# Attention and a gated layer on one core: conversion and attention steps at new places beside chunk 0's first layer, four transfers on GpSimd's queue, and a few sums of weights moved

## The chip, the cores and the metric

The kernel runs on one core of a Trainium2 chip. The metric is the time of one execution on the device, in microseconds. A run of the kernel before takes 1005.83 us (median of 3). The engines are called PE (TensorE), ACT (ScalarE), DVE (VectorE), POOL (GpSimd) and SP (SyncE); each works through its own queue in order.

## The reference

```python
def _attn_ref(q, k, v, g_norm):                       # 8 batches, 8 heads, 576 rows, 64 columns
    kv = np.einsum('bhsd,bhse->bhde', k, v)
    out = np.einsum('bhsd,bhde->bhse', q, kv)
    rms = np.sqrt(np.mean(out * out, axis=-1, keepdims=True) + 1e-06)
    return out / rms * g_norm

def _moe_ref(x, w_gate, w_val, w_out):                # 4608 tokens, 512 wide, 1536 inner
    gate = 1.0 / (1.0 + np.exp(-(x @ w_gate)))
    return (gate * (x @ w_val)) @ w_out
```

The attention's output, brought to 4608 rows of 512, is the `x` of the second part. The weights of the second part come as 64-bit floating point numbers and are read as integers; the kernel turns them into 32-bit floats itself.

## The kernel before

The 4608 tokens are worked on in nine chunks of 512. In each chunk the first layer makes `h` (gate times value, 12 blocks of 128 inner columns) and the second layer makes the output. Chunk 0 does this with plain matrix products. Chunks 1 to 8 use a fast multiplication with fewer products: 26 products for each of three blocks `j` in the first layer (78 in all, `first_layer_fast`, line 957) and 26 in the second (`second_layer_fast`, line 1059). It needs sums of the operands: of `x` (`x_sum`, lines 855 and 857, DVE), of the first layer's weights (`w1_sums(j)`, line 751, 28 sums on POOL for each `j`), of `h` (`h_sums`, line 733, POOL and partly DVE), and of w_out (`w_form(n)`, lines 1030 and 1032, 768 columns each, on DVE or POOL). These sums of weights are made once, beside chunk 0 and chunk 1, and those of the first layer are copied out to memory (`keep_w1`, line 768, one transfer per product, SP's queue) because later chunks load them from there (line 780).

**Chunk 0's first layer.** Its blocks 1 to 11 are 88 "places": place `p` is matmul `p % 8` of block `p // 8 + 1`, each a product of 128x128 by 128x512, which the trace lists as two instructions of line 599. Beside these matmuls a table called `places` hangs other work: `22:CV,CV,C` means that after the matmul of place 22 two conversion steps and the step `C` are issued. Within a place the order is: the matmul, then at the block's places 0 and 2 the two closing steps of the block before (`late`: a sigmoid on ACT called the gate, line 604, and a multiplication on DVE called `end`, line 607), then the steps of the table. As every engine takes its instructions in the order in which they are issued, the table decides what stands ahead of what on ACT, DVE, POOL and SP.

The steps' names:

- `CV` is the next conversion step. Each unit of weights (1024 columns) takes five, on DVE: c`u`.0 (line 197) and c`u`.1 (line 212), each followed by an activation on ACT (lines 202 and 217), then c`u`.2 (224), c`u`.3 (228) and c`u`.4 (235, or 237 for w_out). c`u`.2 needs the first activation, c`u`.3 the second. Some steps also issue a load of later weights on SP's queue. Block `u` of chunk 0 needs unit `u`; units 12 to 17 are w_out, and their remaining steps are issued in chunk 0's second layer (line 833), three in four matmuls.
- `LL` and `LL2` load K and V of batches 1 and 2 into `h_more` (`load_late`, line 134 for the eight large transfers, line 139 for the four small ones of the last 64 rows).
- `KV` and `KV2` multiply K by V of batches 1 and 2 (lines 389 and 396) into a PSUM tile `at`, of which there is one; `C` and `D` copy to `kvq`, `ASIDE` copies `KV2`'s result from PSUM to `kv_ahead` (line 400, ACT).
- `Q0`, `Q1` load q of batch 1 (lines 119 and 120, POOL's queue). `t00` to `t11` turn q on DVE (lines 408 and 410); `t11` issues the twelve q transfers of batch 2 on SP's queue.
- `au`, `asq`, `as0`, `as1`, `art`, `arc`, `an0`, `an1`, `an2`, `ax0`, `ax1` are the attention of the first four heads of batch 1: matmuls into `at` (line 439), square (ACT, 444), two sums (DVE, 447), root (ACT, 450), reciprocal (DVE, 483/485), three groups of six scalings (ACT, 479), two turns (DVE, 462 and 464) with their transfers (SP, 473). `bu` to `bx1` are the same for the other four heads.
- `W0` and `W1` are `w1_sums(0)` and `w1_sums(1)`. They write partly over `h_more`, which `KV2` reads. `w1_sums(2)` follows at the end of the conversions.

In chunk 1 the forms of w_out are issued at fixed products, from a list of (product, form, on POOL or not): `at1` counts the products of the first layer (0 to 77), `at2` those of the second (0 to 25). Form 22 is written over the slots 12 to 14 of block 1's first-layer sums, form 23 into a tile that the profile calls `w_ring`.

Of the kernel before, what the change touches and what calls it, by code (L numbers as in the profile page):

```python
# [20 lines left out]
def kernel(  # L21
# [11 lines left out]
    nc = tc.nc  # L33

    B, H, S, HD = q.shape
# [9 lines left out]
    PH = P // 2  # L45
# [19 lines left out]
    GH = G // 2  # L65
# [59 lines left out]
    def load_late(b):  # L125


        if b >= B:
            return
        mains = {}  # L130
        for n in range(NHP):
            for name, src in (("k", k), ("v", v)):
                mains[n, name] = t = kv_place(len(mains))
                nc.sync.dma_start(out=t.rearrange("p (h c) -> p h c", h=2),  # L134
                                  in_=src[b, 2 * n:2 * n + 2, 0:S4].rearrange("h (p j) d -> p h (j d)", j=NK4))
        rest = kv_place(len(mains))
        for i, src in enumerate((k, v)):
            for r in range(2):
                (nc.sync if b == 1 else nc.scalar).dma_start(out=rest[PH * r:PH * r + PH, GH * i:GH * i + GH].rearrange("p (h d) -> p h d", d=HD),
                                  in_=src[b, NHP * r:NHP * r + NHP, S4:S].rearrange("h p d -> p h d"))  # L140
        kv_late[b] = mains, rest

# [381 lines left out]
    def kv_place(i):  # L524
        return h_more.rearrange("p j s c -> p (j s c)")[:, G * i:G * i + G]
# [98 lines left out]
    KV, KV_OUT, Q, Q_OUT, U, U_SQUARE, U_SUM, U_ROOT, U_NORM, X, X_OUT = range(11)  # L624
# [157 lines left out]
    def w1_form(c, j, part, v):  # L782
        if c == 1:
# [11 lines left out]
    spare_sg = sgs.pop()  # L795
    batch1, second_batch = feed(1), feed(2)
    named = {"LL": lambda: load_late(1), "LL2": lambda: load_late(2), "KV": batch1[0][0], "KV2": second_batch[0][0],
             "W0": lambda: w1_sums(0), "W1": lambda: w1_sums(1),
             "ASIDE": second_batch[0][2], "CV": convert_step}
# [4 lines left out]
    for i, which in enumerate("ab"):  # L804
# [1 line left out]
            named[which + step] = batch1[1][2 * NRUN + 11 * i + n]  # L806
    places = """
        1:CV,CV 2:CV,Q0 4:CV,CV 5:CV,CV 6:CV,LL 7:CV,CV 10:CV,CV 11:Q1 15:CV 16:CV,CV 17:t00
        18:CV,CV 19:t01 20:KV 22:CV,CV,C 25:CV 26:CV,CV 29:au,LL2 30:CV
        31:asq 32:CV,t10,as0 34:CV,as1,art 35:CV 36:t11,arc,an0 37:an1 38:CV,an2 40:CV,CV 41:CV,ax0  # L810
        43:ax1 44:KV2,ASIDE 46:CV,W0 47:bu 48:CV,CV,bsq 50:CV,bs0 52:CV,CV 54:bs1 55:CV,CV,brt,D 57:CV,CV 58:CV 60:CV,brc
        62:bn0,bn1 63:bn2 64:CV 65:CV,CV,CV 66:CV,CV 67:CV 71:bx0 72:CV 74:W1 75:bx1
        80:CV,CV,CV,CV,CV 84:CV 87:CV,CV
    """
    at_place = {}
    for some in places.split():
        p, names = some.split(":")
# [45 lines left out]
    def x_sum(c, n):  # L863
        if c not in x_ops:
            x_ops[c] = x_sums(c)
        x_ops[c][n]()
# [160 lines left out]
    def w_form(v, eng, at_once=True):  # L1027
        sx_, x, sy, y = next(s_[1:] for s_ in W_SUMS if s_[0] == v)
        if sx_ > 0:
            eng.tensor_tensor(out=W_AT[v], in0=W_AT[x], in1=W_AT[y], op=op_of(sy))  # L1030
        else:
            nc.vector.scalar_tensor_tensor(out=W_AT[v], in0=W_AT[x], scalar=-1.0, in1=W_AT[y], op0=ALU.mult,
                                           op1=op_of(sy))
        if v not in STAY:
            stores.append(lambda: nc.sync.dma_start(out=kept3[STREAM.index(v)].rearrange("p (j n) -> p j n", j=N3),
                                                    in_=W_AT[v]))
            if at_once:
                stores.pop()()

    def second_layer_fast(c, at):  # L1040
# [62 lines left out]
        for i in range(1, NPR):  # L1103
            if i != 3:
# [8 lines left out]
                else:  # L1113
                    product(i, blocks)
                    finish(i)
        load_late(c + 2)

    fill.extend(x_early)
# [13 lines left out]
    for c in range(1, NG):  # L1132
        at1, at2 = {}, {}
        for p, step in x_late:
            at1.setdefault(p, []).append(step)
        x_late = []
        if c + 1 < B:
            kv, first_, then = second_batch if c == 1 else feed(c + 1)
            for p, step in (list(zip((21, 22) if c == 2 else (19, 20), kv)) if c > 1 else []) + first_:
                at1.setdefault(p, []).append(step)  # L1140
            for p, step in zip((3, 6) if c == 1 else (4, 6), then):
                at2.setdefault(p, []).append(step)
        if c + 1 < NG:
            for n, p in enumerate(X1 if c == 1 else X2 if c + 1 < B else X3):
                step = lambda n=n, c=c: x_sum(c + 1, n)
                if p < NPR:
                    at2.setdefault(p, []).append(step)
                else:
                    x_late.append((p - NPR, step))
        if c == 1:  # L1150
            for at_, forms in ((at1, ((28, 9, 0), (30, 10, 0), (34, 12, 0), (52, 11, 1), (57, 14, 0), (58, 8, 1), (61, 19, 0), (64, 16, 1))), (at2, ((1, 13, 0), (2, 22, 0), (3, 23, 1), (4, 25, 1), (9, 15, 0), (10, 24, 0), (10, 20, 0), (11, 17, 0), (12, 18, 0), (13, 21, 0)))):
                for p, n, pool_ in forms:
                    at_.setdefault(p, []).append(lambda n=n, eng=nc.gpsimd if pool_ else nc.vector, at_once=at_ is at1 or n == 13: w_form(n, eng, at_once))
        first_layer_fast(c, at1)
        if c == 1:
            sgs += [spare_sg] + more_sgs
        second_layer_fast(c, at2)
# [30 lines left out]
```

## Time and profile before

| | us |
|---|---|
| runs | 1005.83, 1005.03, 1005.9 |
| profiled execution, its own time | 1004.44 |
| its span, first to last instruction | 1002.7 |
| PE busy | 993.8 |
| PEld (weight loads) busy | 815.8 |
| DVE busy | 722.1 |
| ACT busy | 342.5 |
| POOL busy | 617.5 |

The granted clock of TensorE is 1.000 over the whole span. Chunk 0's first layer runs from 22 to 115 us of the span, its second layer to 158 us, chunk 1 to 263 us. In a timeline a row gives the start, the length, the engine, the line, the operation, output and inputs, and in brackets how long the engine had stood idle and who ended that. Rows that follow each other closely with equal names are merged (`x16`). A row of an engine with a `q` (ACTq, SPq, POOLq) is its queue's, which issues transfers.

### The profile page before, as it was taken

How to read it: one execution, taken by the hardware profiler on the slowest of the kernel's cores; microseconds unless marked ns; L12 is line 12 of the kernel's file. 1: busy time of each engine (PE TensorE's matmuls, PEld its weight loads, DVE VectorE, ACT ScalarE, POOL GpSimd, SP SyncE). 2: the span in 40 equal slices, each digit the busy share in tenths (PEclk: the TensorE clock that was granted, in tenths of full speed). 3: DMA queues.
4: the chain of work that ended last, by engine and by line, in shares of the span. 5: the costliest groups of instructions: out<-in, count | busy, mean ns of one | idle time of the engine just before them, and what ended most of it. 6: DMA issues, size and time to landing. Idle time of an engine off the chain costs nothing.

```text
span 1002.7 us, 16624 instructions
## 1 busy us (share of the span) xinstructions
PE 993.8 (99%) x5958; PEld 815.8 (81%) x5958; DVE 722.1 (72%) x1198; ACT 342.5 (34%) x606; POOL 617.5 (62%) x988
## 2 busy tenths in 40 slices
PE   8999999999999999999999999999999999999998
PEld 7455447888888888888888888888888888888887
DVE  4989999889757756784677676866587566755672
ACT  4566332562144213530344124421342133213320
POOL 1509997798359633965186707861595449744963
PEclk9999999999999999999999999999999999999999
DMA  9995414673799568846875577755864555444514
GB/s 271 269 265 183 172 51 115 215 236 127 248 301 272 176 189 240 239 156 203 257 240 171 181 223 237 203 171 179 258 201 141 167 173 211 156 149 162 214 53 122
DMA packets 156114, 195.43 MB, mean 195 GB/s; under 512 B 84832, under 2 KB 128864, under 8 KB 156032
## 3 DMA queue, kind: packets, MB, share of 16 engines
q0 software_dynamic: 22000, 114.11, 34.4%
q1 hardware_dynamic: 126864, 78.16, 27.6%
q10 hardware_dynamic: 7168, 2.10, 0.9%
q8 instruction: 47, 0.77, 0.3%
q14 instruction: 35, 0.29, 0.1%
HBM read 160.50 MB, written 25.56 MB: 186 GB/s over the span
## 4 chain that ended last, share of the span: by engine, by line
PE 73%; POOL 2%; DMA 1%; issue 0%; SPq 0%; DVE 0%; POOLq 0%
PE mm L957 46%; PE mm L1059 24%; PE at L439 1%; POOL h L733 1%; PE at L389 1%; DMA h_more<-in_v_dram 1%; POOL w_ring L1030 0%; POOL h_more L733 0%; PE at L396 0%; SPq L134 0%; POOL w L780 0%; DVE sg L927 0%; POOLq L780 0%; POOLq L1030 0%
## 5 line engine op out<-in xcount | busy, mean ns | idle before, releaser
L957 PE MATMUL mm<-xs,w 128*128 128x256 f32 x1428 | 331.8, 380 | 0.0
L957 PEld LDWEIGHTS mm<-xs,w 128*128 128x128 f32 x1428 | 270.5, 190 | 37.1
L957 PE MATMUL mm<-xT,w 128*128 128x256 f32 x948 | 229.8, 380 | 0.0
L957 PEld LDWEIGHTS mm<-xT,w 128*128 128x128 f32 x948 | 179.5, 190 | 25.0 <-issue 0.5
L780 POOL DMA_DIRECT2D w<-kept x84 | 46.8, 557 | 189.4 <-PE mm L957 187.3
L927 DVE TENSOR_TENSOR sg<-sg,mm 128x512 f32<-128x512 f32 (+1 forms) x176 | 100.7, 599 | 85.5 <-PE mm L957 41.5
L1059 PE MATMUL mm<-w,h 128*128 128x256 f32 x630 | 143.1, 379 | 0.3 <-POOL h L733 0.3
L1059 PEld LDWEIGHTS mm<-w,h 128*128 128x128 f32 x630 | 119.6, 190 | 17.0 <-POOL h L733 0.7
L919 POOL TENSOR_TENSOR h<-h,sg 128x512 f32<-128x512 f32 x72 | 96.0, 1350 | 57.0 <-DVE h L927 31.0
L923 ACT COPY temps<-mm 128x512 f32<-128x512 f32 (+1 forms) x128 | 66.0, 538 | 186.9 <-PE mm L1059 94.7
L733 POOL TENSOR_TENSOR h<-h 128x128 f32<-128x128 f32 x216 | 112.1, 531 | 16.6 <-DVE h_more L733 13.1
L1059 PE MATMUL mm<-w,h_more 128*128 128x256 f32 x474 | 108.2, 379 | 0.0
L916 ACT ACTIVATE sg<-sg 128x512 f32<-128x512 f32 x96 | 59.7, 630 | 131.5 <-DVE sg L927 131.5
L1059 PEld LDWEIGHTS mm<-w,h_more 128*128 128x128 f32 x474 | 90.1, 190 | 12.2
L923 ACT COPY sg<-mm 128x512 f32<-128x512 f32 (+1 forms) x112 | 56.9, 510 | 86.5 <-PE mm L1059 45.0
L733 POOL TENSOR_TENSOR h_more<-h 128x128 f32<-128x128 f32 x120 | 61.6, 517 | 34.3 <-DVE h L919 30.0
L927 DVE TENSOR_TENSOR temps<-temps,mm 128x512 f32<-128x512 f32 (+1 forms) x96 | 59.4, 619 | 25.9 <-PE mm L1059 16.6
L599 PE MATMUL mm<-xT,w 128*128 128x512 f32 x176 | 77.8, 596 | 0.1
L927 DVE TENSOR_TENSOR temps<-mm,temps 128x512 f32<-128x512 f32 (+1 forms) x64 | 39.8, 622 | 50.9 <-PE mm L1059 23.6
L923 ACT COPY h<-mm 128x512 f32<-128x512 f32 x48 | 28.1, 585 | 140.4 <-PE mm L957 126.4
L927 DVE TENSOR_TENSOR sg<-mm,sg 128x512 f32<-128x512 f32 (+1 forms) x64 | 39.7, 620 | 45.1 <-PE mm L957 24.5
L599 PEld LDWEIGHTS mm<-xT,w 128*128 128x128 f32 x176 | 32.6, 190 | 39.2 <-issue 36.8
(145 smaller groups left out, 1284.2 us busy)
## 6 DMA issues: line engine op xcount, KB each, us to landing
w<-kept POOLq DMA_DIRECT2D x42, 896.0 KB, 5.7
w<-kept POOLq DMA_DIRECT2D x90, 384.0 KB, 4.6
w<-kept POOLq DMA_DIRECT2D x42, 768.0 KB, 5.5
out_dram<-sg SPq DMA_DIRECT2D x119, 64.0 KB, 1.7
h_more<-in_k_dram SPq DMA_DIRECT2D x28, 256.0 KB, 5.6
h_more<-in_v_dram SPq DMA_DIRECT2D x28, 256.0 KB, 6.5
q<-in_q_dram SPq DMA_DIRECT2D x96, 72.0 KB, 5.0
xT<-xTs SPq DMA_DIRECT2D x96, 72.0 KB, 4.4
```

The costliest lines, as they stand in the source:

```text
L389: nc.tensor.matmul(ps[HD * g:HD * g + HD, m, e], mains[2 * m + g, "k"][:, c], mains[2 * m + g, "v"][:, c], start=(e == 0 and j == 0), stop ...
L439: nc.tensor.matmul(u[HD * e:HD * e + HD, o:o + HD], qTs[HD * g:HD * g + HD, c:c + HD], kvq[HD * g:HD * g + HD, t == NSL, m, e], start=True ...
L599: nc.tensor.matmul(self.ps[i], w[("wg", "wv")[i], self.f][:, m, :], xT[self.c][:, m, :], start=(m == 0), stop=(m == NMT - 1), skip_group_c ...
L733: ops.append((eng, lambda v=v, x=x, sign=sign, y=y, eng=eng: eng.tensor_tensor(out=h_form(v, j), in0=h_form(x, j), in1=h_form(y, j), op=op ...
L780: nc.gpsimd.dma_start(out=granule(g)[:, 0:n], in_=kept1[g // NPA % N3, g % NPA][:, 0:n])
L916: nc.scalar.activation(out=o["o" + step[1]], in_=o["o" + step[1]], func=AF.Sigmoid)
L919: mult.tensor_tensor(out=o[x], in0=o[x], in1=o[y], op=ALU.mult)
L923: nc.scalar.copy(out=o[out_], in_=o[expr])
L927: tt(out=o[out_], in0=o[x], in1=o[y], op=ALU.add if sign == "+" else ALU.subtract)
L957: nc.tensor.matmul(regions[name][1][:, g], ws[:, g], xf[c][wv], start=(new and g == 0), stop=True, skip_group_check=True)
L1059: nc.tensor.matmul(regions[name][1], h_form(hv, j), ws[:, j], start=(used[i] and j == 0), stop=(j == N3 - 1), skip_group_check=True)
```

## The change

- `load_late(2)`: the four small transfers are issued on POOL's queue; before, on ACT's. The other batches stay as they are.
- The table `places`, between places 30 and 55, and 74 and 87: `t10` goes from 32 to 33, `as0` from 32 to 34, `as1` and `art` from 34 to 35, `t11` and `arc` from 36 to 37, `an0` from 36 to 38, `an1` from 37 to 41, `an2` from 38 to 43, `ax0` from 41 to 45, `ax1` from 43 to 46, `KV2` and `ASIDE` from 44 to 47, `W0` from 46 to 49, `bu` from 47 to 50, `bsq` from 48 to 51, `bs0` from 50 to 53, `bs1` from 54 to 55, and `W1` from 74 to 87. The conversion steps keep their number and their order among themselves; c6.3 to c9.0 get other places (c6.3 32 to 30, c7.1 38 to 35, c7.2 40 to 37, c8.0 46 to 43, c8.1 48 to 45, c8.2 48 to 50, for instance).
- Form 22 of w_out goes from product 2 of chunk 1's second layer to product 53 of its first layer, on DVE as before. Form 23 stays at product 3 of the second layer and goes from POOL to DVE.

```diff
-                (nc.sync if b == 1 else nc.scalar).dma_start(out=rest[PH * r:PH * r + PH, GH * i:GH * i + GH].rearrange("p (h d) -> p h d", d=HD),
+                (nc.sync if b == 1 else nc.gpsimd if b == 2 else nc.scalar).dma_start(out=rest[PH * r:PH * r + PH, GH * i:GH * i + GH].rearrange("p (h d) -> p h d", d=HD),
...
-        18:CV,CV 19:t01 20:KV 22:CV,CV,C 25:CV 26:CV,CV 29:au,LL2 30:CV
-        31:asq 32:CV,t10,as0 34:CV,as1,art 35:CV 36:t11,arc,an0 37:an1 38:CV,an2 40:CV,CV 41:CV,ax0
-        43:ax1 44:KV2,ASIDE 46:CV,W0 47:bu 48:CV,CV,bsq 50:CV,bs0 52:CV,CV 54:bs1 55:CV,CV,brt,D 57:CV,CV 58:CV 60:CV,brc
-        62:bn0,bn1 63:bn2 64:CV 65:CV,CV,CV 66:CV,CV 67:CV 71:bx0 72:CV 74:W1 75:bx1
-        80:CV,CV,CV,CV,CV 84:CV 87:CV,CV
+        18:CV,CV 19:t01 20:KV 22:CV,CV,C 25:CV 26:CV,CV 29:au,LL2 30:CV,CV
+        31:asq 32:CV 33:t10 34:as0,CV 35:as1,art,CV 37:t11,CV,arc 38:an0 40:CV 41:an1 42:CV 43:an2,CV 45:CV,ax0
+        46:ax1 47:KV2,ASIDE 49:W0 50:CV,bu 51:CV,bsq 52:CV 53:bs0,CV 55:bs1,CV,CV,brt,D 57:CV,CV 58:CV 60:CV,brc
+        62:bn0,bn1 63:bn2 64:CV 65:CV,CV,CV 66:CV,CV 67:CV 71:bx0 72:CV 75:bx1
+        80:CV,CV,CV,CV,CV 84:CV 87:CV,CV,W1
...
-            for at_, forms in ((at1, ((28, 9, 0), (30, 10, 0), (34, 12, 0), (52, 11, 1), (57, 14, 0), (58, 8, 1), (61, 19, 0), (64, 16, 1))), (at2, ((1, 13, 0), (2, 22, 0), (3, 23, 1), (4, 25, 1), (9, 15, 0), (10, 24, 0), (10, 20, 0), (11, 17, 0), (12, 18, 0), (13, 21, 0)))):
+            for at_, forms in ((at1, ((28, 9, 0), (30, 10, 0), (34, 12, 0), (52, 11, 1), (53, 22, 0), (57, 14, 0), (58, 8, 1), (61, 19, 0), (64, 16, 1))), (at2, ((1, 13, 0), (3, 23, 0), (4, 25, 1), (9, 15, 0), (10, 24, 0), (10, 20, 0), (11, 17, 0), (12, 18, 0), (13, 21, 0)))):
```

## The prediction

> **What bounds the kernel now.** I read the page first, then PE's waits, PE's timeline, and last the timelines of ACT, DVE and POOL around chunk 0's first layer (22 to 115 us). The page:
>
> ```profile
> PE 993.8 (99%) x5958; PEld 815.8 (81%) x5958; DVE 722.1 (72%) x1198; ACT 342.5 (34%) x606; POOL 617.5 (62%) x988
> ```
>
> PE is busy 993.8 of 1002.7 us. The change adds and removes no matmul, so only the holes in PE's work can shrink or grow. PE's list of waits names them; behind the start-up these three are left (total us, times, longest):
>
> ```profile
> PE mm L833 <- DVE w L237: 0.7, 3, 0.4
> PE mm L1059 <- POOL h L733: 0.3, 1, 0.3
> PE at L389 <- DMA h_more<-in_v_dram: 0.2, 1, 0.2
> ```
>
> The holes are larger in PE's timeline (start us, length us; idle before it in brackets):
>
> ```profile
> 108.68 7.03 PE L599 MATMUL at<-xT,w 128*128 128x512 f32 x16
> 116.06 7.10 PE L833 MATMUL mm<-w,h 128*128 128x512 f32 x16 [0.35 <-DVE w L237]
> 123.38 7.13 PE L833 MATMUL mm<-w,h 128*128 128x512 f32 x16 [0.21 <-DVE w L237]
> 130.67 27.73 PE L833 MATMUL mm<-w,h 128*128 128x512 f32 x64 [0.16 <-DVE w L237]
> ```
>
> The last row gives 27.73 / 64 = 0.433 us a matmul (its last one ends late; start to start it is 0.429). Sixteen are 6.87, but the starts lie 7.38, 7.32 and 7.29 apart: 0.51 + 0.45 + 0.42 = 1.38 us lost, all to the conversion of w_out on DVE. So in chunk 0 DVE is the engine that is late, from about 84 us on. The windows (PE, PEld, DVE, ACT, POOL busy) show it at its limit:
>
> ```profile
> 100.00:120.00 20.00, 19.65 (x46) 8.47 (x45) 19.80 (x21) 8.59 (x10) 19.61 (x16) 1.00 0.53 177
> 120.00:140.00 20.00, 19.63 (x46) 8.38 (x45) 19.74 (x17) 6.76 (x6) 19.76 (x17) 1.00 0.28 105
> ```
>
> What DVE loses before 84 us therefore comes back as a PE hole of the same size after 100 us. That is the question of this change. The most it can win is 1.38 us there and the hole at 253 us.
>
> **The steps around place 47.** ACT, then DVE, then POOL, before the change:
>
> ```profile
> 60.15 2.15 ACTq L139 DMA_DIRECT2D h_more<-in_v_dram  x2
> 62.35 1.13 ACT L444 ACTIVATE sqs<-at 128x1152 f32<-128x1152 f32 x1 [3.08 <-DMA h_more<-in_k_dram]
> 77.16 0.37 ACT L400 COPY kv_ahead<-at 128x256 f32<-128x256 f32 x1 [2.04 <-PE at L396]
> ```
>
> ```profile
> 72.02 1.22 DVE L228 SCALAR_TENSOR_TENSOR cz<-st,cz 128x1024 uint32<-128x1024 uint32 x1 [2.00 <-ACT cz L217]
> ...
> 78.70 1.59 DVE L224 SCALAR_TENSOR_TENSOR w<-st,w 128x1024 f32<-128x1024 uint32 x1
> 80.21 0.68 DVE L607 TENSOR_TENSOR h<-mm,sg 128x512 f32<-128x512 f32 x1
> ```
>
> ```profile
> 75.39 0.73 POOL L751 TENSOR_TENSOR h_more<-w 128x256 f32<-128x256 f32 x1 [34.70 <-DVE xTs L464]
> ...
> 111.46 1.70 POOL L751 TENSOR_TENSOR h_more<-w 128x256 f32<-128x256 f32 x1
> ```
>
> **Four transfers to POOL's queue.** ACT's queue issues them until 62.30 us; the `au` matmuls end at 61.62, so `asq` gains 0.7 us. On POOL they fall into its idle time from 41 to 75 us: its 16 transfers of q issued at 24.7 to 40 us took 0.70 us each, so four cost 2.8 us; they wait only for the first batch's `KV`, over at 52.4, and land long before `KV2`. Behind them stands W0, which cannot start before 75 us anyway. Cost nothing, with 20 us of cover; gain 0 to 0.7 us, counted in the walk. The Trainium skill (SBUF — State Buffer, "SBUF: two separate sides") speaks against this move: VectorE in a two-port mode locks GpSimd out of writing descriptors, so such a transfer waits. The rows of q above were issued beside a DVE busy 17.94 of 20 us and show no large wait; by that page of the Trainium skill the landing is late, but into the same cover, so the sum would be equal.
>
> **The order of steps, walked with the rows' durations** (DVE pitch: two-tensor conversion steps 1.14 to 1.20, the single-tensor ones 0.60, `end` 0.60, sums 0.66, a pair of x turns 0.75; ACT: conversion 1.05, gate 0.5, table load 1.28, root 0.2, six norms 1.27). c6.2, c6.3, c6.4 run on to 61.7, t10 to 62.4; `end` at 34 waits for the gate (asq to 62.75, gate to 63.3): 63.4. Then as0, c7.0, as1, c7.1, t11 to 67.4, c7.2 to 68.5, arc to 68.7. ACT: c7.0's half to 66.4, table load and root to 67.9, c7.1's half to 69.0, an0 to 70.3, table load and gate to 72.0. c7.3 ends at 70.2, but `end` at place 42 now stands between an0 and an1 and waits for that gate: DVE idle 2.0 us, the size of the 2.00 row above. From 72.2: `end`, c7.4, c8.0, c8.1, ax0, ax1, to 76.7 us. ACT's an2 is done by 74.6, before `KV2` wants the PSUM tile at 77.2, so PE is not held.
>
> Then the cost. `KV2` moves from place 44 to 47: three places of 0.866 us, so it ends at 79.7 instead of 77.1. ACT's order is kv_ahead, gate; DVE's is now `end` (place 50), c8.2. The copy ends at 80.1, the gate at 80.7, and `end` starts at 80.75: DVE idles 4.0 us. Before, c8.0 to c8.2 stood ahead of that `end` and filled this wait. At 80.21 `end` stood with c8.2 done; now at 80.75 c8.2 (1.51 pitch) is still to come, less the 0.43 idle before bs0 that it fills: 0.54 + 1.51 - 0.43 = 1.6 us late at c9.1. From there the order is the old one and DVE is full, so 1.6 stays. I look for it as a hole at place 72 (before, `end` of block 8 freed its banks at 101.47 and PE came at 101.9: 1.2 us) and the rest at the first w_out pair. Bounds: 0.9 (c8.2 and c8.3 at 1.2, a gate earlier) to 2.2.
>
> **W0 three places later, W1 thirteen.** W0 follows `KV2`: 78.0 instead of 75.4. W1's first sum starts at 111.46 with no idle before it, right behind W0's last, and no other POOL instruction lies between places 74 and 87: W1's new place moves nothing. Its own start goes with W0's end, at most 2.6 us; its results are wanted at chunk 1's product 26, near 180 us, and POOL idles 7.07 us at 170 to 177. Nothing. SP's queue keeps its order (c7.2's load stays behind t11's twelve q transfers).
>
> **Two sums of w_out.** POOL's chain runs without a pause into PE's hole at 253 us:
>
> ```profile
> 237.20 2.53 POOL L1030 TENSOR_TENSOR w_ring<-w,w 128x768 f32<-128x768 f32 x1
> ...
> 253.27 3.07 PE L1059 MATMUL mm<-w,h 128*128 128x256 f32 x13 [0.33 <-POOL h L733]
> ```
>
> That row is form 23; on DVE it takes the slot of form 22 (1.21 us at 236.84), so DVE is level there and POOL 2.5 us ahead: the hole goes, 0.50 us start to start plus 0.1 at the restart. Next late is the V transfer at 283 us, behind stores that move with PE: no change, or at worst all of the 0.6 is lost there. Form 22 at product 53 (1.2 us) falls behind the x turns, where DVE idles 2.40 us before 210.59. It overwrites slots 12 to 14 of block 1, whose last copy out is issued at 205.27; these land in 2.3 us, so 207.6 to 208, as DVE arrives at 208.1. Cost 0, to 1 us if that copy is late.
>
> **Sum.** +1.6 - 0.6 = +1.0 us on the profiled execution: 1004.44 (span 1002.7 and 1.74 around it) becomes 1005.4. The median of the runs lies 1.39 above the profiled one, so I say 1006.8. A measurement of this kernel tells about 0.2%, 2 us, from no change: this is within it. The case's own range, 0.9 - 0.6 to 2.2 - 0, is 1006.1 to 1008.0.
>
> **Rivals.** *Slower: POOL wins the contention.* While W0 runs, DVE's L224 takes 1.635 us on the mean against 1.213 before 75.4 us. But c8.3, c8.4 and c9.0 (80.8 to 85.5) still took 1.21 to 1.28, while POOL's sums beside them took 1.2 to 1.77 instead of 0.73. If DVE, starting 0.5 us later into a W0 that has had 2.7 us to itself, is the loser there from the start, these three take 1.7: +1.5 us, 3.1 late, 2.5 after POOL's gain: 1008.3. It decides from 2.6 us late at c9.1. For it: every long step from 86.75 on is of that size; against: nothing fixes who starts first. The same section of the Trainium skill's page (SBUF — State Buffer) says that whoever starts first holds the port pair for the whole instruction; the rows of 0.73 against 1.2 agree in kind.
>
> *Faster: DVE is not late.* If the gate at 48 did not hold `end`, or the freed 3.08 us of ACT and the 2.00 us wait count in full, DVE comes 1.4 us early, and all holes go: -1.38 - 0.6 = -2.0, 1003.8. For it: those waits are real rows. Against: the kv_ahead copy stands ahead of the gate in ACT's order.
>
> *The w_out sums cost.* The copy out of slot 14 is late by 2 us or more, DVE stands at product 53 and product regions come free late: 1008 and more.
>
> *Nothing moves:* if the 4 us are filled as before and POOL's gain is eaten at 283 us: 1005.8.
>
> **How the numbers follow.** Forecast 0.47, POOL wins 0.25, faster 0.13, w_out sums cost 0.06, nothing 0.09. Of the forecast a tenth lies above 1007.8. Slower: 0.25 + 0.06 + 0.04 = 0.35; same: 0.43 + 0.09 = 0.52; faster 0.13. The range goes from the faster case to the slower one with the 0.6 lost as well: 1003.8 to 1009.0.
>
> **What would show it.** Right: DVE idle some 4 us before L607 near 80.7 us, W0 starting near 78, ACT's L444 near 61.7 without a wait on a transfer, PE holes at L599 near 102 us, no wait on POOL near 253. Wrong: L607 near 80.2 with L224 ahead of it, PE's three waits on L237 gone, W1 not directly behind W0, or DVE idle before L1030 near 208 us.

## The result and the profile after

| | before | after |
|---|---|---|
| median of 21 runs each, us | 1005.47 | 1006.83 |
| ratio, 95% interval | | 1.0017 [1.0010, 1.0025] |
| profiled execution, own time / span, us | 1004.44 / 1002.7 | 1006.54 / 1004.8 |
| first `au` matmul (L439) to chunk 1's first L957, us | 98.00 | 100.33 |
| chunk 1's first L957 to chunk 2's first, us | 104.63 | 104.67 |

By the medians the change costs 1.4 us, by the ratio 1.7; both are inside the 0.2% that the prediction calls no change, and the interval leaves out 1. Two executions of the experiments, at a granted clock of 0.751 (1304.68 us, places_only) and 0.85 (1156.03 us, queue_only), are left out of all ratios. Between the two profiled executions the span grows by 2.1 us: 2.33 in chunk 0 behind `au`, 0.04 in chunk 1, 0.27 in the later chunks, less 0.54 that the first `au` matmul comes earlier (59.70 instead of 60.24 us). The engines' line of the page hardly moves, since the same work is done:

```profile
PE 994.2 (99%) x5958; PEld 815.6 (81%) x5958; DVE 722.3 (72%) x1199; ACT 342.2 (34%) x606; POOL 616.3 (61%) x991
```

PE's list of waits (total us, times, longest) has two new releasers in chunk 0, the gate on ACT and L235 on DVE; the wait on the conversion of w_out (L237) has grown from 0.7 to 1.3. The wait on POOL's sums of `h` is still there, now at L957 instead of L1059:

```profile
PE mm L833 <- DVE w L237: 1.3, 3, 1.0
...
PE at L599 <- DVE w L235: 0.8, 1, 0.8
PE at L389 <- DMA h_more<-in_v_dram: 0.5, 1, 0.5
PE mm L599 <- ACT sg L604: 0.4, 1, 0.4
PE mm L957 <- POOL h L733: 0.4, 1, 0.4
```

PE's timeline shows where they lie:

```profile
101.88 7.13 PE L599 MATMUL mm<-xT,w 128*128 128x512 f32 x16 [0.44 <-ACT sg L604]
109.78 7.11 PE L599 MATMUL at<-xT,w 128*128 128x512 f32 x16 [0.76 <-DVE w L235]
117.85 7.10 PE L833 MATMUL mm<-w,h 128*128 128x512 f32 x16 [0.97 <-DVE w L237]
125.17 7.13 PE L833 MATMUL mm<-w,h 128*128 128x512 f32 x16 [0.21 <-DVE w L237]
132.46 27.73 PE L833 MATMUL mm<-w,h 128*128 128x512 f32 x64 [0.15 <-DVE w L237]
...
229.23 1.10 PE L957 MATMUL mm<-xs,w_ring 128*128 128x256 f32 x4 [0.41 <-POOL h L733]
...
254.34 6.64 PE L1059 MATMUL mm<-w,h 128*128 128x256 f32 x30
```

From start to start, less the pitch of 0.429 us, the chunk 0 holes are 0.60, 0.92, 1.14, 0.38 and 0.32 us: 3.35. The same count for before gives 0.52, 0.37 and 0.32: 1.21. (The prediction's 1.38 for before also counts the slow first matmul behind a hole, some 0.1 us.) At 253 us no row stands with a wait any more; a new one stands at 229. The window from 100 to 120 us says the same, PE down from 19.65 to 17.83 of 20 with DVE as full as before:

```profile
100.00:120.00 20.00, 17.83 (x41) 7.35 (x40) 19.86 (x20) 8.56 (x15) 19.61 (x16) 1.00 0.58 174
```

The steps around place 47, in the timelines of ACT, DVE and POOL:

```profile
61.13 1.13 ACT L444 ACTIVATE sqs<-at 128x1152 f32<-128x1152 f32 x1 [2.57 <-PE at L439]
...
79.20 0.37 ACT L400 COPY kv_ahead<-at 128x256 f32<-128x256 f32 x1 [2.42 <-PE at L396]
79.47 0.60 ACT L604 ACTIVATE sg<-mm 128x512 f32<-128x512 f32 x1
```

```profile
72.07 0.69 DVE L607 TENSOR_TENSOR h<-mm,sg 128x512 f32<-128x512 f32 x1 [1.91 <-ACT sg L604]
...
80.11 0.69 DVE L607 TENSOR_TENSOR h<-mm,sg 128x512 f32<-128x512 f32 x1 [3.48 <-ACT sg L604]
80.72 1.37 DVE L224 SCALAR_TENSOR_TENSOR w<-st,w 128x1024 f32<-128x1024 uint32 x1
82.01 1.76 DVE L228 SCALAR_TENSOR_TENSOR cz<-st,cz 128x1024 uint32<-128x1024 uint32 x1
83.81 1.63 DVE L235 SCALAR_TENSOR_TENSOR w<-w,g_col,cz 128x1024 f32<-128x1024 f32 x1
```

```profile
52.14 1.25 POOL L139 DMA_DIRECT2D h_more<-in_k_dram  x2 [11.01 <-PE at L396]
53.39 1.23 POOL L139 DMA_DIRECT2D h_more<-in_v_dram  x2
...
77.43 0.73 POOL L751 TENSOR_TENSOR h_more<-w 128x256 f32<-128x256 f32 x1 [22.82 <-PE at L389]
...
112.12 1.17 POOL L751 TENSOR_TENSOR h_more<-w 128x256 f32<-128x256 f32 x1
```

`end` of block 6 (the L607 at 80.11) now stands ahead of c8.2 (L224). It waits for the gate, the gate stands behind the copy to `kv_ahead` in ACT's order, and the copy needs `KV2`: DVE idles 3.48 us. The four transfers lie in POOL's idle time. W1 (112.12) follows W0 with no idle time between.

### The profile page after: what moved, and what is told of

It is laid out like the page before. It is cut to its first block, busy times and chain, and to the rows that moved or that the text cites. A ratio compares the mean times of both kernels' runs of the same rounds, so it can differ in the third digit from the quotient of the medians.

```text
span 1004.8 us, 16622 instructions
## 1 busy us (share of the span) xinstructions
PE 994.2 (99%) x5958; PEld 815.6 (81%) x5958; DVE 722.3 (72%) x1199; ACT 342.2 (34%) x606; POOL 616.3 (61%) x991
## 4 chain that ended last, share of the span: by engine, by line
PE 88%; DVE 5%; POOL 2%; ACT 2%; DMA 2%; issue 1%; SPq 1%; DVEq 0%; POOLq 0%; ACTq 0%
PE mm L957 49%; PE mm L1059 27%; PE mm L599 5%; PE mm L833 3%; PE at L439 2%; PE at L389 1%; DMA h_more<-in_v_dram 1%; DVE cz L228 1%; DVE w L224 1%; POOL h_more L733 1%; DVE w L197 1%; POOL h L733 1%; DMA v<-in_v_dram 1%; POOL h L919 0%; POOL w L1030 0%
## 5 line engine op out<-in xcount | busy, mean ns | idle before, releaser
L957 PE MATMUL mm<-xs,w 128*128 128x256 f32 x1428 | 331.8, 380 | 0.0
L957 PEld LDWEIGHTS mm<-xs,w 128*128 128x128 f32 x1428 | 270.5, 190 | 37.1
L957 PE MATMUL mm<-xT,w 128*128 128x256 f32 x948 | 229.8, 380 | 0.0
L957 PEld LDWEIGHTS mm<-xT,w 128*128 128x128 f32 x948 | 179.5, 190 | 25.0 <-DMA out_dram<-sg 0.2
L927 DVE TENSOR_TENSOR sg<-sg,mm 128x512 f32<-128x512 f32 (+1 forms) x176 | 100.7, 599 | 86.2 <-PE mm L957 42.3
L1059 PE MATMUL mm<-w,h 128*128 128x256 f32 x630 | 142.8, 379 | 0.0
L1059 PEld LDWEIGHTS mm<-w,h 128*128 128x128 f32 x630 | 119.7, 190 | 16.3
L919 POOL TENSOR_TENSOR h<-h,sg 128x512 f32<-128x512 f32 x72 | 96.7, 1360 | 57.6 <-DVE h L927 31.1
L733 POOL TENSOR_TENSOR h<-h 128x128 f32<-128x128 f32 x216 | 112.1, 531 | 16.5 <-DVE h_more L733 13.1
L1059 PE MATMUL mm<-w,h_more 128*128 128x256 f32 x474 | 108.2, 379 | 0.0
L1059 PEld LDWEIGHTS mm<-w,h_more 128*128 128x128 f32 x474 | 90.1, 190 | 12.2
L733 POOL TENSOR_TENSOR h_more<-h 128x128 f32<-128x128 f32 x120 | 61.6, 517 | 34.3 <-DVE h L919 30.0
L599 PE MATMUL mm<-xT,w 128*128 128x512 f32 x176 | 78.0, 597 | 0.5 <-ACT sg L604 0.4
L927 DVE TENSOR_TENSOR temps<-temps,mm 128x512 f32<-128x512 f32 (+1 forms) x96 | 59.3, 618 | 26.2 <-PE mm L1059 16.9
L927 DVE TENSOR_TENSOR temps<-mm,temps 128x512 f32<-128x512 f32 (+1 forms) x64 | 39.8, 622 | 50.8 <-PE mm L1059 23.9
L927 DVE TENSOR_TENSOR sg<-mm,sg 128x512 f32<-128x512 f32 (+1 forms) x64 | 39.6, 619 | 46.1 <-PE mm L957 24.0
L599 PEld LDWEIGHTS mm<-xT,w 128*128 128x128 f32 x176 | 32.5, 190 | 40.0 <-issue 35.9
```

Source lines behind the costliest of these rows:

```text
L599: nc.tensor.matmul(self.ps[i], w[("wg", "wv")[i], self.f][:, m, :], xT[self.c][:, m, :], start=(m == 0), stop=(m == NMT - 1), skip_group_c ...
L733: ops.append((eng, lambda v=v, x=x, sign=sign, y=y, eng=eng: eng.tensor_tensor(out=h_form(v, j), in0=h_form(x, j), in1=h_form(y, j), op=op ...
L919: mult.tensor_tensor(out=o[x], in0=o[x], in1=o[y], op=ALU.mult)
L927: tt(out=o[out_], in0=o[x], in1=o[y], op=ALU.add if sign == "+" else ALU.subtract)
L957: nc.tensor.matmul(regions[name][1][:, g], ws[:, g], xf[c][wv], start=(new and g == 0), stop=True, skip_group_check=True)
L1059: nc.tensor.matmul(regions[name][1], h_form(hv, j), ws[:, j], start=(used[i] and j == 0), stop=(j == N3 - 1), skip_group_check=True)
```

## The experiments

All are timed against the kernel before on the same chip. The last two columns are from each kernel's trace, one execution each; PE's clock in them was granted at 0.999 to 1.000. The trace for places_only is that of places_look, the same kernel.

| kernel | ratio, 95% interval | L439 to L957, us | chunk 1, us |
|---|---|---|---|
| before | | 98.00 | 104.63 |
| after | 1.0017 [1.0010, 1.0025] | 100.33 | 104.67 |
| places_only | 1.0015 [1.0006, 1.0024] | 100.37 (places_look) | 104.63 |
| queue_only | 1.0000 [0.9991, 1.0009] | 98.66 | 104.62 |
| forms_only | 0.9988 [0.9980, 0.9997] | 98.61 | 104.68 |
| form23_only | 0.9995 [0.9986, 1.0004] | 98.78 | 104.03 |
| after_22_back | 1.0011 [1.0001, 1.0021] | 100.33 | 104.02 |
| after_kv45 | 1.0006 [0.9998, 1.0015] | 100.06 | 104.67 |
| after_fill3 | 1.0006 [0.9997, 1.0016] | 99.42 | 104.67 |
| after_fill5 | 0.9984 [0.9975, 0.9994] | 97.18 | 104.68 |
| early | 0.9963 [0.9950, 0.9976] | 96.51 | 104.03 |

### The three parts, each alone

places_only and places_look are the kernel before with the whole new table:

```diff
-        31:asq 32:CV,t10,as0 34:CV,as1,art 35:CV ... 43:ax1 44:KV2,ASIDE 46:CV,W0 ... 74:W1 75:bx1
+        31:asq 32:CV 33:t10 34:as0,CV 35:as1,art,CV ... 46:ax1 47:KV2,ASIDE 49:W0 50:CV,bu ... 87:CV,CV,W1
```

> The kernel before with the new table of places alone. Theory (DVE waits before the end of block 6 and stays late): DVE idle 3 to 4 us before L607 near 80 us, PE holes at L599 near 102 and 110 us and at L833, together some 2 us larger than before, the hole on POOL near 253 us still there (0.6), no hole near 229: +2.0 us, 1.002 of before. Rival (the forms of w_out make the difference, by the hole at 229 us): no slower than before, within 0.5 us.

> The kernel before with the new table of places alone, looked at for its trace. Theory: DVE idle 3.5 us before L607 near 80 us, c9.2 starts 28.8 us after the first au matmul (27.05 where the places are the old ones), PE's holes at 101, 108 and 116 us as in the kernel after, no hole at 229 us, the hole at 253 us as before. Rival (the four transfers or the sums of w_out share in the holes of chunk 0): smaller holes at 101 to 116 us.

queue_only:

```diff
-(nc.sync if b == 1 else nc.scalar)
+(nc.sync if b == 1 else nc.gpsimd if b == 2 else nc.scalar)
```

> The kernel before with the four transfers of batch 2 on POOL's queue alone. Theory: square L444 of the first four heads starts with the end of its matmuls, 0.6 us earlier, DVE's wait before the sums shrinks by as much, the holes of 1.4 us at 116 to 131 us shrink by at most 0.6 us: -0.6 to 0 us. Rival (transfers written by POOL are held up by DVE and make KV2 late): a hole at L389 near 75 us, slower by its length.

forms_only:

```diff
-(52, 11, 1), (57, 14, 0) ... (1, 13, 0), (2, 22, 0), (3, 23, 1)
+(52, 11, 1), (53, 22, 0), (57, 14, 0) ... (1, 13, 0), (3, 23, 0)
```

> The kernel before with the two moved sums of w_out alone (form 22 at product 53, form 23 on DVE). Theory: the hole at 253 us (0.6 us with its restart) goes and one of 0.7 us opens near 229 us, because form 22 holds POOL up and POOL's form 11 then lies beside DVE's L1032: net 0.0 to +0.2 us. Rival (the hole at 229 us comes from the late DVE of chunk 0): no hole at 229, -0.6 us.

The table alone gives the slowdown of the whole change: 1.0015 against 1.0017, and a chunk 0 of 100.37 against 100.33 us. PE's timeline of places_look has the same first three holes at the same steps:

```profile
102.02 7.13 PE L599 MATMUL mm<-xT,w 128*128 128x512 f32 x16 [0.49 <-ACT sg L604]
109.92 7.10 PE L599 MATMUL at<-xT,w 128*128 128x512 f32 x16 [0.77 <-DVE w L235]
118.00 7.10 PE L833 MATMUL mm<-w,h 128*128 128x512 f32 x16 [0.98 <-DVE w L237]
```

The four transfers are worth nothing that can be measured (1.0000 [0.9991, 1.0009]). How long they hold ACT's square up differs between the traces that still have them on ACT: it starts 1.49 us behind `au` in forms_only, 2.11 in before, 2.62 in form23_only and 3.07 in places_look, against 1.43 where they are on POOL. Of the 1.19 us between form23_only and queue_only 0.12 are left at c9.2 (27.17 and 27.05 us behind `au`), and of the 1.64 between places_look and after 0.03 (28.80 and 28.77). So the gain on ACT is absorbed ahead of the steps that are late. In places_look it is DVE's wait ahead of `end` that absorbs it: 2.17 us, where 3.5 was expected, and `end` still comes 20.41 us behind `au`, as in after. DVE's timeline of places_look:

```profile
80.19 0.69 DVE L607 TENSOR_TENSOR h<-mm,sg 128x512 f32<-128x512 f32 x1 [2.17 <-ACT sg L604]
```

So the length of that idle time is not the cost: with 3.48 us and with 2.17 chunk 0 is as late.

The four traces with the old table (before, forms_only, queue_only, form23_only) have 98.00, 98.61, 98.66 and 98.78, 98.5 on the mean. None of the three edits touches c8.3 (L228) or c8.4 (L235), and yet in DVE's timelines of before (given first) and of forms_only c8.4 has another length:

```profile
80.81 1.21 DVE L228 SCALAR_TENSOR_TENSOR cz<-st,cz 128x1024 uint32<-128x1024 uint32 x1
...
83.12 1.28 DVE L235 SCALAR_TENSOR_TENSOR w<-w,g_col,cz 128x1024 f32<-128x1024 f32 x1
```

```profile
80.78 1.21 DVE L228 SCALAR_TENSOR_TENSOR cz<-st,cz 128x1024 uint32<-128x1024 uint32 x1
...
83.20 1.82 DVE L235 SCALAR_TENSOR_TENSOR w<-w,g_col,cz 128x1024 f32<-128x1024 f32 x1
```

c8.4 starts 22.88 us behind `au` in both. POOL's next sum (L751) starts at 23.02 in before, and at 22.90 in forms_only. So the profiled execution of before was the fortunate one of the four by 0.6 to 0.8 us, and the rows put it down to who comes first of DVE and POOL. Against the mean of the four, the table costs 100.35 - 98.5 = 1.8 us.

### The two sums of w_out, taken apart

after_22_back takes form 22 back to product 2, and leaves form 23 on DVE; form23_only is the kernel before with the list that this gives:

```diff
-(53, 22, 0), ... (1, 13, 0), (3, 23, 0)
+(1, 13, 0), (2, 22, 0), (3, 23, 0)
```

> The kernel after with form 22 issued at product 2 of the second layer again (form 23 stays on DVE at product 3). Theory (form 22 at product 53 shifts POOL's form 11 beside DVE's L1032 and so opens the hole at 229 us): that hole (0.7 us with its restart) is gone, form 14's L1032 takes 1.2 us instead of 1.95, and the hole at 253 us does not come back, as POOL stays 2.5 us ahead: -0.7 us against the kernel after. Rival (the hole at 229 us comes from moving form 23 or from chunk 0's lateness): it stays, no change.

> The kernel before with form 23 on DVE alone; form 22 stays at product 2 of the second layer. Theory: the hole at 253 us goes (0.6 us with its restart), none opens at 229 us, chunk 1 takes 104.0 us of PE time instead of 104.6, chunk 0 as before: -0.6 us, 0.9994. Rival (DVE, full from 232 to 252 us, hands its sums over late with one form more): a new hole in the second layer, no gain.

They have a chunk 1 of 104.02 and 104.03 us (as early has below), 0.6 below all the others: form 23 on DVE is worth the 0.6 us that was predicted, and form 22 at product 53 takes them away. This stands in the traces; the ratios (0.9995 [0.9986, 1.0004] for form23_only) cannot tell 0.6 us from nothing. The timelines show how. First after, DVE and POOL, then after_22_back, DVE and POOL:

```profile
210.10 1.01 DVE L1030 TENSOR_TENSOR w<-w,w 128x768 f32<-128x768 f32 x1
...
213.71 1.95 DVE L1032 SCALAR_TENSOR_TENSOR w<-w,w 128x768 f32<-128x768 f32 x1
```

```profile
207.40 4.85 POOL L919 TENSOR_TENSOR h<-h,sg 128x512 f32<-128x512 f32 x3
...
213.03 1.81 POOL L1030 TENSOR_TENSOR w<-w 128x768 f32<-128x768 f32 x1
```

```profile
213.97 1.23 DVE L1032 SCALAR_TENSOR_TENSOR w<-w,w 128x768 f32<-128x768 f32 x1
```

```profile
207.66 4.12 POOL L919 TENSOR_TENSOR h<-h,sg 128x512 f32<-128x512 f32 x3
...
212.56 1.82 POOL L1030 TENSOR_TENSOR w<-w 128x768 f32<-128x768 f32 x1
```

Form 22 (the L1030 at 210.10) fits into DVE's idle time, as predicted. But it runs beside POOL's three multiplications L919, which take 4.85 instead of 4.12 us. POOL's own form 11 then starts 5.63 us behind the first of them instead of 4.90, and lies for 1.13 us instead of 0.41 beside DVE's next form (L1032), which takes 1.95 instead of 1.23. From there DVE has hardly a pause until the merges (L927) that free the PSUM tiles for the second layer, and PE has a hole of 0.57 us at 229, and 0.1 at the restart. Without form 22 no wait stands there. That form 22's place decides whether the hole is there is shown by the two pairs of traces (with it: after and forms_only; without: after_22_back and form23_only). That it reaches PE through DVE is read from the rows: the last merge ahead of the hole ends at 229.09, 0.14 us before PE goes on, as c11.4 ends 0.15 us before PE goes on at 109.78. The list of waits names POOL's L733, which ends at 229.19. Counted from the start of chunk 1, DVE and POOL are both 0.68 us later there than in after_22_back, and no run parts the two.

### Where the 3.48 us could be filled

after_kv45 moves `KV2` two places forward. after_fill3 puts c8.2 to c8.4 ahead of `end`, into the idle time. after_fill5 also puts c9.0 and c9.1 ahead of `bs0` (the line that it takes out is that of after_fill3):

```diff
 after_kv45
-45:CV,ax0 46:ax1 47:KV2,ASIDE 49:W0
+45:CV,ax0,KV2,ASIDE 46:ax1 49:W0
 after_fill3
-46:ax1 47:KV2,ASIDE 49:W0 50:CV,bu 51:CV,bsq 52:CV 53:bs0,CV 55:bs1,CV,CV,brt,D
+46:ax1,CV,CV,CV 47:KV2,ASIDE 49:W0 50:bu 51:bsq 53:bs0,CV 55:bs1,CV,CV,brt,D
 after_fill5
+46:ax1,CV,CV,CV 47:KV2,ASIDE 49:W0 50:bu 51:bsq,CV,CV 53:bs0 55:bs1,CV,brt,D
```

> The kernel after with KV2 and ASIDE at place 45 instead of 47, all else as it is. Theory (the end of block 6 waits for the kv_ahead copy behind KV2): KV2 ends 1.7 us earlier, L607 starts near 79.0 instead of 80.1 us (then bound by the matmul of place 47), DVE is 1.0 us earlier after it and PE's first matmul of w_out 0.5 to 1.0 us earlier: -0.5 to -1.0 us. Rival (DVE's pace beside W0 is all that counts): W0 also starts 1.7 us earlier, and nothing is won.

> The kernel after with c8.2, c8.3 and c8.4 issued at place 46, ahead of the end of block 6 (before: places 50, 51, 52). Theory (DVE's wait there is the whole loss): the 3.5 us idle before L607 near 80 us is filled, DVE is 3 us earlier from there, the holes at 102, 110 and 118 to 132 us vanish but for 0.5 us; -2.5 to -3 us against the kernel after, -1.5 us against before. Rival (POOL's sums beside DVE set its pace, the order does not matter): the three steps take 1.7 us each beside W0 and at most 1 us is won.

> The kernel after with c8.2, c8.3, c8.4 at place 46 and also c9.0, c9.1 at place 51, ahead of the sums bs0. In the run with the first three alone, DVE's 3.5 us before L607 were gone but 2.8 us of idle time came back before bs0. Theory (DVE's work before 88 us is the whole matter; the idle time only has to be filled): the wait before bs0 falls to 1 us or less, c9.2 starts near 87 us, 1.0 us earlier than there, holes at 108 us gone, at 115 us halved: -1.0 us against the run with three. Rival (DVE and POOL share, and DVE's steps lengthen by what they start earlier): less than 0.3 us.

after_kv45: `end` comes 0.7 us earlier behind `au` (19.74 instead of 20.41 us), but c8.2 falls beside W0's start and takes 1.72 instead of 1.37. Only 0.27 us arrive at chunk 1, where 0.5 to 1.0 was expected: the longer c8.2 takes half of what `end` gains. DVE's timeline:

```profile
81.59 0.69 DVE L607 TENSOR_TENSOR h<-mm,sg 128x512 f32<-128x512 f32 x1 [2.81 <-PE mm L599]
82.20 1.72 DVE L224 SCALAR_TENSOR_TENSOR w<-st,w 128x1024 f32<-128x1024 uint32 x1
```

after_fill3 took the idle time of 3.48 us away, and won 0.9 us in the trace, where 2.5 to 3 was expected. That is the number of its rival (the three steps take 1.7 us each beside W0 and at most 1 us is won), and c8.3 and c8.4 did take 1.75 and 1.63 us. But in after they take as long (1.76 and 1.63), so their length is not what was not won. DVE's timeline shows a new wait of 2.81 us at the next step that depends on PE:

```profile
81.55 0.68 DVE L607 TENSOR_TENSOR h<-mm,sg 128x512 f32<-128x512 f32 x1
85.03 0.76 DVE L447 TENSOR_REDUCE ms<-sqs 128x9 f32<-128x576 f32 x1 [2.81 <-ACT sqs L444]
```

`bs0` needs `bsq`, which needs `bu` at place 50. DVE was ready before it, and the conversion steps that could have filled this wait stand behind it. after_fill5 puts two of them there. DVE's idle time falls to 1.06 us, the holes in front of L599 go, and so do those at w_out apart from 0.16 and 0.31 us (DVE, then PE):

```profile
84.75 1.41 DVE L447 TENSOR_REDUCE ms<-sqs 128x9 f32<-128x576 f32 x2 [1.06 <-ACT sqs L444]
```

```profile
108.42 7.03 PE L599 MATMUL at<-xT,w 128*128 128x512 f32 x16
115.29 20.14 PE L833 MATMUL mm<-w,h 128*128 128x512 f32 x45
```

(The last row shows the matmuls up to 135 us only.) Chunk 0 is 3.1 us shorter than in after and 2.2 shorter than in after_fill3, where 1.0 was expected, and the kernel is faster than before (0.9984 [0.9975, 0.9994]). c8.3 and c8.4 take 1.75 and 1.63 us here too, so it is the order and not their length that wins this. With the attention steps left at their new places, the cost of the new table is won back by what stands behind the waiting steps. What the later attention steps cost by themselves was not tried alone.

### early: all that gained, and a fuller order

The old table has waits of the same kind (c7.3 2.00 us on c7.1's activation, `bs0` 0.43 us on its square). early takes the kernel before, the four transfers on POOL's queue, form 23 on DVE with form 22 left at product 2, and brings conversion steps ahead of the steps that wait:

```diff
-34:CV,as1,art 35:CV ... 38:CV,an2 40:CV,CV 41:CV,ax0 43:ax1 44:KV2,ASIDE 46:CV,W0 47:bu 48:CV,CV,bsq 50:CV,bs0 52:CV,CV 54:bs1 55:CV,CV,brt,D
+34:CV,as1,art 35:CV,CV ... 38:an2 40:CV,CV 41:CV,CV,CV,ax0 43:ax1,CV 44:KV2,ASIDE 46:W0,CV 47:bu,CV 48:bsq 50:CV,bs0 52:CV 54:bs1 55:CV,brt,D
```

> The kernel before with its own places of KV2 and of the attention steps, but c7.1 ahead of the six-fold scalings, c8.0 to c8.4 and c9.0 issued ahead of the waits they stood behind, the four transfers on POOL, form 23 on DVE, form 22 as before. Theory: DVE's waits of 2.0, 0.8 and 0.5 us between 70 and 83 us are filled, c9.1 starts 1.5 to 2 us earlier, PE's holes before the w_out matmuls shrink from 1.4 to 2.1 us to below 0.5, the hole at 253 us is gone and none is at 229 us: -2 us against before, 0.998. Rival (POOL's contention takes back what DVE starts earlier): holes at 116 us as before, -0.6 us by POOL's sum alone.

Its median (five runs) is 1002.43 us against 1005.0 for the kernel before, 2.6 us less; the ratio, 0.9963 [0.9950, 0.9976], says 2.4 to 5.0. It is faster than before, and before is faster than after. PE's timeline has no hole left in chunk 0 from 81 us to the end of w_out; the one row of L833 holds the 96 matmuls that before stood in three rows with waits:

```profile
80.70 27.73 PE L599 MATMUL mm<-xT,w 128*128 128x512 f32 x64
108.27 7.03 PE L599 MATMUL at<-xT,w 128*128 128x512 f32 x16
115.14 41.36 PE L833 MATMUL mm<-w,h 128*128 128x512 f32 x96
```

The trace accounts for 2.0 us in chunk 0 (98.5 to 96.51) and 0.6 in chunk 1: the 2.6 of the medians, at the low end of the interval. The transfers alone gave nothing and form 23 the 0.6, so the 2.0 are put down to the order. Two of DVE's waits stay, 0.76 us ahead of an `end` and 0.69 ahead of `bs0`.

## Why the prediction was right, and where it was not

**The number: right, in part by luck.** 1006.8 was forecast and 1006.83 measured. The forecast put the profiled execution at 1005.4 and the median 1.39 us above it. The profiled execution took 1006.54, and the median lies 0.29 above it. So 1.1 us too little for the change and 1.1 too much for that distance cancel. Against the median of 21 runs before, 1005.47, the change is +1.4 (by the ratio 1.7), where the sum said +1.0.

**`KV2` and `end`: right in mechanism; the lateness behind them was put too low.** `end` was walked to 20.51 us after the first `au` matmul (80.75 - 60.24) and came at 20.41; W0 to 17.76 and came at 17.73. DVE's idle time ahead of `end` was put at 4.0 and measured 3.48; the one ahead of the L607 at 72 us at 2.0 and measured 1.91. DVE is late at c9.1 by 2.27 us against the profiled execution of before (87.84 - 59.70 against 86.11 - 60.24), and by 1.7 at c9.2 against the other three traces of the old table (28.77 us behind `au` instead of 27.05 to 27.17). The walk said 1.6, with bounds of 0.9 and 2.2, and it was made on the profiled execution of before: there 2.27 lies just outside, and so do the 2.33 us by which chunk 0 is longer. What was put too low is c8.3 and c8.4, which the walk left at 1.21 and 1.28 us and which took 1.76 and 1.63; c8.2 took 1.37 instead of 1.59. Against the other traces of the old table the 1.7, and chunk 0's 1.8 over the mean, lie inside the bounds.

**Where the lateness comes out: the place was right, the shares were wrong.** It was to be 1.2 us in front of place 72, by `end` of block 8, and the rest at w_out. The first hole is 0.60 us and the gate ends it: the L604 at 101.10 stands behind eighteen scalings that take ACT 3.77 us. A second of 0.92 us ends with c11.4 (L235), and w_out's first grows to 1.14 (0.52 in before, but 1.13 to 1.15 in the other three traces of the old table). Here the late DVE showed at every step that PE takes from it, and not at the first one alone.

**The four transfers, W1, SP's queue: right, nothing.** They took 1.25 + 1.23 us in a POOL idle for 11.01 us, and alone they changed no median. ACT's square came 1.43 us after `au`, 1.46 by the walk. The Trainium skill (SBUF — State Buffer, "SBUF: two separate sides") warns that a transfer issued from GpSimd can starve while VectorE runs in a two-port mode. Here two of them took 1.25 us beside a DVE with no pause from 49 to 56 us, so no run here shows that delay; in which mode those steps of DVE ran, the traces do not say.

**The sums of w_out: the step that failed.** The term was -0.6 us. The hole at 253 went, as said, and another of the same size came at 229: the two together are +0.04. Form 22 was costed at 0 because DVE is idle there, and at up to 1 us "if that copy is late". The copy was not late; what was left out is that POOL works beside that idle time, and that a sum on DVE lengthened POOL's three multiplications by 0.73 us. The bound covered the size, not the cause. So the terms that the runs support are +1.8 and about 0, where the sum had +1.6 and -0.6.

**Rival "POOL wins the contention": partly.** c8.3 and c8.4 did take 1.76 and 1.63 us in after; c9.0 stayed at 1.24, so two of the rival's three steps grew. For c8.3 this comes with the order: 1.21 us in each of the four traces of the old table, 1.74 to 1.76 in each of the seven with another order. For c8.4 it does not: it took 1.82 in forms_only, 1.81 in queue_only and 1.77 in form23_only, with the old table. There it is a difference between executions of some 0.5 us, and the profiled execution of before was on the good side of it. The same section of the Trainium skill (SBUF — State Buffer) says that whoever starts first holds the port pair for the whole instruction. The traces agree in kind, in that DVE's instruction grows by some 0.5 us, less than the 0.73 of a whole sum of POOL.

**Left open.** forms_only was measured 1.2 us faster [0.3, 2.0], though its trace shows nothing gained in chunks 0 and 1. From chunk 2 on PE's work takes the same time in every trace but for a wait of `KV` on the transfer of V, which is 0 in six of them, 0.39 in form23_only, 0.51 in before, 0.84 in after, 1.0 in early and 2.4 us in places_look. (These are lengths over the pitch, so they lie above the listed waits.) The time up to the first `au` matmul, which no edit touches, runs from 59.70 us (after) to 61.85 (after_kv45). Both vary by as much as is to be explained; what sets them was not tried.

## What to carry to other kernels

Before a step that waits is moved in an order written by hand, list the steps behind it on the same engine: the wait costs the time in which they could have run, and filling one such gap only uncovers the next wait unless the fillers are spread (0.9 us for three steps in one place, 3.1 for five in two). An idle slot on VectorE is not free while GpSimd works beside it: look at both engines' rows for the slot. Where two engines contend, take several traces of the same order before differences of half a microsecond are charged to an edit.

## What the runs showed of the hardware

The same conversion step on VectorE (c8.4) beside GpSimd's sums took 1.28 us in one execution and 1.77 to 1.82 in three others with its neighbours in the order unchanged: the order of arrival is not fixed by the program. One sum of 128x768 on VectorE lengthened three multiplications of GpSimd by 0.73 us together (4.12 to 4.85), and that lateness brought a further 0.72 us on VectorE's next form (1.23 to 1.95): one meeting set up the next.
